# Attention states by one VectorE scan over single-chunk products, in place of two partial sums

## The chip, the core and the metric

The kernel runs on one core of a Trainium2 chip. The metric is the device time of one execution in microseconds. The kernel before takes 101.39 us, the median of three runs (101.31 to 101.42).

## The reference, cut to what matters

Two stages follow each other: a causal linear attention with decay over 32 heads (4 batches of 8), and a token mixer over its output. The change touches only the attention's running state.

```python
batch, n_heads, seq, head_dim = (4, 8, 768, 64)
block = 64
...
for b in range(nb):
    qb, kb, vb = q[:, :, sl], k[:, :, sl], v[:, :, sl]
    intra = (einsum(qb, kb) * Dmask) @ vb
    inter = einsum('bhid,bhde->bhie', qb * lam_pow, kv_state)
    out[:, :, sl] = intra + inter
    kb_dec = kb * rev_pow
    kv_state = lam_block * kv_state + einsum('bhsd,bhse->bhde', kb_dec, vb)
...
# x: the attention's output as (batch, seq, 512)
wq, wk = x @ w_q, x @ w_k
mixed = ((wq @ wk.T) / 8) @ x
result = relu(mixed) @ w_out
```

The state at a block is a sum over all earlier blocks. The kernel uses chunks of 128 tokens, so a head has 6 chunks, and 5 states are needed: chunk c + 1 reads the sum of the products of chunks 0 to c. The decay is put into q and v as powers of lambda that count from the start of the sequence. No factor then stands between one state and the next: the states are plain prefix sums of the products k^T v.

## The kernel before

Two heads make a pair; pair n has its first head on partitions 0 to 63 and its second on 64 to 127 (`R[0]`, `R[1]`). There are 16 pairs. The whole program is one long list of pieces in a fixed order, each with its operands and PSUM banks; `P.6@3` is the piece P of pair 6 in bank 3, and `:a`, `:v` or `:p` names ScalarE, VectorE or GpSimd. The list sets each engine's order. A cut of it, where the first two of the ten pairs stand (lines joined):

```python
ORDER = """
...
m.0.2@3@0 eh.0.2.0@3:a F.4@4 ek.6@2:a eh.0.2.1@0:v P.6@3 P.5@5 Gp.6@3 eh.0.3.0@1:a S0.6@6 O.0.4@2
Gp.5@5 Mc.0.6@6 ef.4@4:v S1.6@6 eo.0.4@2:a I.6@0 Mm.0.6:v I.5@4 V.5@4 M1.6@6 Aq.7@2 ex.5@4:a
...
"""
```

For a pair the pieces are: A and e turn q and k, S multiplies them into scores, M or Mc with Mm masks them, sv scales v, P makes the products for the states, G or Gp brings them to SBUF as states, I multiplies q with the states, V adds the masked scores times v, ex takes the result out, F and ef turn it. Q, K, Y, m, O with their e pieces are the mixer.

There are two ways to the states. With `Pw` (6 of the 16 pairs: 0 to 4 and 14) TensorE forms all prefix sums: the product of chunk c is added to all states from c on, and G is one copy. With `P` (the other ten pairs) only the first two products are summed so, and apart from them the last three; VectorE then adds the state at place 1 to the last three.

```python
    def states(whole):
        def one(n, o):
            to = PS[:, o, 0 : (NCH - 1) * D].rearrange("e (c f) -> e c f", c=NCH - 1)
            for c in range(NCH - 1):
                end = 2 if c < 2 and not whole else NCH - 1
                for hl in range(2):
                    mm(
                        to[R[hl], c:end, :],
                        fk[n][:, hl, c, :],
                        vn[n][:, hl, c, :].unsqueeze(1).to_broadcast([128, end - c, D]),
                        start=(c == 0), stop=(c == NCH - 2), skip_group_check=True,
                    )
        return one
...
    def added(n, o):
        gs[n] = tsb.tile([128, NCH - 1, D], BF16, tag="gs", name="gs")
        of = PS[:, o, 0 : (NCH - 1) * D].rearrange("e (c f) -> e c f", c=NCH - 1)
        two = small.tile([128, 1, D], F32, tag="two", name="two")
        nc.vector.tensor_copy(out=two, in_=of[:, 1:2, :])
        nc.vector.tensor_copy(out=gs[n][:, 0:2, :], in_=of[:, 0:2, :])
        nc.vector.tensor_tensor(
            out=gs[n][:, 2:, :], in0=of[:, 2:, :],
            in1=two.to_broadcast([128, NCH - 3, D]), op=ALU.add,
        )

    def inter(n, o):
        for c in range(1, NCH):
            for hl in range(2):
                mm(
                    PS[:, o + hl, c * D : (c + 1) * D],
                    qT[n][R[hl], c * CH : (c + 1) * CH],
                    gs[n][R[hl], c - 1, :],
                    start=(c == 1), stop=False, skip_group_check=True,
                )
```

In `mm` the second argument holds the weights and the third streams through. So a pair's P has ten products, five for each head, of 128, 64, 192, 128 and 64 columns. Scaling of v (sv) is on VectorE for seven pairs and on GpSimd for nine. GpSimd also issues the loads. One scan is in the kernel already, at its start, over 128 elements in SBUF:

```python
    nc.vector.tensor_tensor_scan(
        out=ET[:, 0:CH], data0=step, data1=step, initial=0.0, op0=ALU.add, op1=ALU.bypass
    )
```

Of the kernel before, what the change touches and what calls it, by code (L numbers as in the profile page):

```python
# [9 lines left out]
BF16 = mybir.dt.bfloat16  # L10
F32 = mybir.dt.float32
ALU = mybir.AluOpType
ACT = mybir.ActivationFunctionType

B, H, S, D = 4, 8, 768, 64
CH = 128
NCH = S // CH
HD = H * D
DHY = 64
NP = H // 2  # L20
HALF = 3 * CH
N = B * NP
R = (slice(0, 64), slice(64, 128))
# [16 lines left out]
Aq.5@4 Ak.5@5 ek2.0.1@1:v ek2.0.0@0:a Mm.1.4:v Y.0@0 ek.5@5:a eq.5@4 YA.0@0:a YB.0@0:v S1.5@4  # L40
M1.5@4 YC.0@0:a m.0.1@1@2 Pw.4@3 eh.0.1.1@2:a m.0.0@0@6 eh.0.1.0@1:v G.4@3:a Aq.6@2 eh.0.0.1@6:a
I.4@4 eq.6@2 eh.0.0.0@0:a S0.5@6 m.0.3@1@3 M0.5@6 V.4@4 eh.0.3.1@3:a Ak.6@2 ex.4@4:a sv.6:v
m.0.2@3@0 eh.0.2.0@3:a F.4@4 ek.6@2:a eh.0.2.1@0:v P.6@3 P.5@5 Gp.6@3 eh.0.3.0@1:a S0.6@6 O.0.4@2
Gp.5@5 Mc.0.6@6 ef.4@4:v S1.6@6 eo.0.4@2:a I.6@0 Mm.0.6:v I.5@4 V.5@4 M1.6@6 Aq.7@2 ex.5@4:a
Ak.7@3 eq.7@2 O.0.5@6 ek.7@3:v V.6@0 eo.0.5@6:v S1.7@2 S0.7@4 M1.7@2 F.5@6 O.0.0@7 ex.6@0:v
O.0.3@2 eo.0.0@7:a M0.7@4 O.0.1@7 ef.5@6:v F.6@3 sv.8:v eo.0.1@7:a P.7@6 Ak.8@4 ef.6@3:a Gp.7@6
Aq.8@7 P.8@5 ek.8@4:a eq.8@7 I.7@0 V.7@0 Gp.8@5 Aq.9@4 ex.7@0:a eo.0.3@2:v Ak.9@5 S0.8@6 ek.9@5:v
S1.8@2 Mc.0.8@6 F.7@0 eq.9@4 O.0.2@5 ef.7@0:v Mc.1.8@2 Mm.0.8:v Q.1.0@4 eo.0.2@5:a Mm.1.8:v
Q.1.1@2 eQ.1.0@4:a S1.9@4 eQ.1.1@2:a S0.9@0 I.8@6 M1.9@4 Mc.0.9@0 P.9@3 K.1@2 V.8@6 Gp.9@3
eK.1@2:a ex.8@6:a Y.1@2 Mm.0.9:v Ak.10@3 YA.1@2:v YB.1@2:a Aq.10@6 ek.10@3:v YC.1@2:a I.9@0  # L50
eq.10@6 m.1.1@4 m.1.2@2 em.1.1@4:a V.9@0 em.1.2@2:v Aq.11@6 ex.9@0:a P.10@7 eq.11@6 m.1.0@2
S0.10@4 Gp.10@7 m.1.3@0 em.1.0@2:a F.9@6 M0.10@4 Ak.11@7 em.1.3@0:a Aq.12@2 Ak.12@3 ef.9@6:a
ek.11@7:v eq.12@2 S1.11@4 ek.12@3:a S0.11@0 S1.10@6 M0.11@0 O.1.1@2 Mc.1.11@4 M1.10@6 O.1.3@3
eo.1.1@2:a Mm.1.11:v P.11@2 eo.1.3@3:a Ak.13@6 Gp.11@2 Aq.13@7 ek.13@6:a S0.12@4 eq.13@7 I.11@2
I.10@0 Mc.0.12@4 V.11@2 V.10@0 ex.11@2:v O.1.4@4 ex.10@0:a Mm.0.12:v F.8@5 eo.1.4@4:a F.11@0
O.1.5@1 ef.8@5:a ef.11@0:v F.10@0 eo.1.5@1:a S1.13@4 ef.10@0:v S0.13@2 S1.12@6 Mc.0.13@2 M1.13@4
Q.2.0@0 Mc.1.12@6 Q.2.1@1 Mm.0.13:v eQ.2.0@0:a P.13@4 Mm.1.12:v Ak.15@5 eQ.2.1@1:a Gp.13@4 Aq.15@0
ek.15@5:a Ak.14@1 eq.15@0 Aq.14@4 ek.14@1:a sv.15:v K.2@6 Pw.14@0 eK.2@6:a S0.15@2 eq.14@4 P.12@1
Mc.0.15@2 Y.2@5 Gp.12@1 G.14@0:a P.15@4 YB.2@5:v YA.2@5:a I.13@2 S1.15@0 Gp.15@4 S0.14@6 YC.2@5:a
V.13@2 Mc.0.14@6 M1.15@0 O.1.0@4 ex.13@2:a Mm.0.14:v I.15@0 S1.14@6 Mm.0.15:v eo.1.0@4:a I.12@2  # L60
V.12@2 M1.14@6 V.15@0 ex.12@2:a I.14@4 ex.15@0:v m.2.3@6 V.14@4 F.12@2 em.2.3@6:v ex.14@4:a F.15@3
F.13@0 ef.12@2:a ef.15@3:v F.14@1 m.2.1@6 ef.13@0:v ef.14@1:a m.2.0@4 m.2.2@2 em.2.0@4:v O.1.2@0
# [9 lines left out]
def kernel(  # L72
# [11 lines left out]
    nc = tc.nc  # L84
    mm = nc.tensor.matmul

    consts = ctx.enter_context(tc.tile_pool(name="consts", bufs=1))
    stage = ctx.enter_context(tc.tile_pool(name="stage", bufs=N))
    tsb = ctx.enter_context(tc.tile_pool(name="tsb", bufs=4))
    small = ctx.enter_context(tc.tile_pool(name="small", bufs=2))  # L90
    big = ctx.enter_context(tc.tile_pool(name="big", bufs=2))
# [4 lines left out]
    PS = ps.tile([128, 8, HD], F32, name="ps")  # L96
    PSH = PS.bitcast(BF16)
# [42 lines left out]
    def load_wo(_):  # L140
# [28 lines left out]
        out=ET[:, 0:CH], data0=step, data1=step, initial=0.0, op0=ALU.add, op1=ALU.bypass  # L169
    )  # L170
    for at, n in ((CH, CH), (2 * CH, 2 * CH), (4 * CH, 2 * CH)):
        nc.vector.tensor_tensor(
            out=ET[:, at : at + n], in0=ET[:, 0:n],
# [3 lines left out]
    ident = consts.tile([128, 128], BF16, name="ident")  # L177
    nc.vector.tensor_tensor(
        out=ident.rearrange("e (p r) -> e p r", r=2), in0=natural,
# [4 lines left out]
        out=mask1, in0=ET[:, 0:CH], in1=row.to_broadcast([128, CH]), op=ALU.is_ge  # L184
# [4 lines left out]
    for r in range(2):  # L189
        nc.vector.tensor_tensor(  # L190
            out=token[R[r], :], in0=token[R[r], :],
# [5 lines left out]
        out=order.rearrange("e (p r) -> e p r", r=2), in0=natural,  # L197
# [5 lines left out]
        out=E6, in0=ET[:, ::CH], in1=row.to_broadcast([128, NCH]), op=ALU.add  # L203
# [3 lines left out]
    lamv = lam_all.rearrange("p (k l) -> p k l", l=2)  # L207
    for hl in range(2):
        nc.scalar.activation(out=lncol[R[hl], :], in_=lamv[R[hl], :, hl], func=ACT.Ln)
    pw48 = consts.tile([128, H, NCH], F32, name="pw48")  # L210
    mask2 = mask1.unsqueeze(1).unsqueeze(1).to_broadcast([128, 2, 3, CH])
    Dq = [consts.tile([128, S], BF16, name=f"dq{kk}") for kk in range(NP)]
# [18 lines left out]
    qT, kT, pr, gs = {}, {}, {}, {}  # L231
    xnat, xT = {}, {}
# [97 lines left out]
    def masked(a):  # L330
        def one(n, o):
            pr[n, a] = tsb.tile([128, 2, HALF], BF16, tag=f"pr{a}", name="pr")
            nc.vector.tensor_tensor(  # L333
                out=pr[n, a].rearrange("j l (c i) -> j l c i", c=3),
                in0=PS[:, o : o + 2, 0:HALF].rearrange("j l (c i) -> j l c i", c=3),
                in1=mask2,
                op=ALU.mult,
            )

        return one  # L340
# [10 lines left out]
        )  # L351


    def states(whole):
        def one(n, o):
            to = PS[:, o, 0 : (NCH - 1) * D].rearrange("e (c f) -> e c f", c=NCH - 1)
            for c in range(NCH - 1):
                end = 2 if c < 2 and not whole else NCH - 1
                for hl in range(2):
                    mm(  # L360
                        to[R[hl], c:end, :],
                        fk[n][:, hl, c, :],
                        vn[n][:, hl, c, :].unsqueeze(1).to_broadcast([128, end - c, D]),
                        start=(c == 0),
                        stop=(c == NCH - 2),
                        skip_group_check=True,
                    )

        return one

    def summed(n, o, eng):
        gs[n] = tsb.tile([128, NCH - 1, D], BF16, tag="gs", name="gs")
        of = PS[:, o, 0 : (NCH - 1) * D].rearrange("e (c f) -> e c f", c=NCH - 1)
        copy(eng, gs[n], of)

    def added(n, o):
        gs[n] = tsb.tile([128, NCH - 1, D], BF16, tag="gs", name="gs")
        of = PS[:, o, 0 : (NCH - 1) * D].rearrange("e (c f) -> e c f", c=NCH - 1)
# [4 lines that stand above are left out]
            out=gs[n][:, 2:, :],  # L383
            in0=of[:, 2:, :],
            in1=two.to_broadcast([128, NCH - 3, D]),
            op=ALU.add,
        )

    def inter(n, o):
        for c in range(1, NCH):  # L390
            for hl in range(2):
                mm(
                    PS[:, o + hl, c * D : (c + 1) * D],
                    qT[n][R[hl], c * CH : (c + 1) * CH],
                    gs[n][R[hl], c - 1, :],
                    start=(c == 1),
                    stop=False,
                    skip_group_check=True,
                )
# [24 lines left out]
    def flip(n, o):  # L424
        b, kk = divmod(n, NP)
        for c in range(NCH):
            nc.tensor.transpose(  # L427
                PSH[:, o, c * CH : (c + 1) * CH],
                xnat[b][:, c, kk * CH : (kk + 1) * CH],
                order,  # L430
            )

    def flipped(n, o, eng):
# [10 lines left out]
    qk, wkn, YA, YB, rmT = {}, {}, {}, {}, {}  # L444
# [24 lines left out]
            qk[b] = small.tile([128, S], BF16, tag="qk", name="qk")  # L469
        copy(eng, qk[b][:, n * HALF : (n + 1) * HALF], PS[:, o, 0:HALF])  # L470

    def mix_k(b, o, chunks=range(NCH)):
        for c in chunks:
            for r in range(2):
                mm(
                    PS[R[r], o, c * DHY : (c + 1) * DHY],
                    qk[b][:, c * CH + r : (c + 1) * CH : 2],
                    ident[:, R[1 - c // 3]],
                    start=(c == chunks[0]),
                    stop=(c == chunks[-1]),  # L480
                    skip_group_check=True,
                )

    def mix_k_half(b, half, o):
        mix_k(b, o, range(3 * half, 3 * half + 3))
# [47 lines left out]
    def relu(eng, to, of):  # L533
        if eng == "a":
            nc.scalar.activation(out=to, in_=of, func=ACT.Relu, scale=1.0 / 8.0)  # L535
        else:
            nc.vector.tensor_scalar(
                out=to, in0=of, scalar1=1.0 / 8.0, scalar2=0.0, op0=ALU.mult, op1=ALU.max
            )

    def mixed_m(b, dd, o, eng):
        if b not in rmT:
            rmT[b] = big.tile([128, 4, 2, HALF], BF16, tag="rmT", name="rmT")
        relu(eng, rmT[b][:, dd], PS[:, o : o + 2, 0:HALF])

    def mixed_m_half(b, dd, n, o, eng):
        if b not in rmT:
            rmT[b] = big.tile([128, 4, 2, HALF], BF16, tag="rmT", name="rmT")
        relu(eng, rmT[b][:, dd, n], PS[:, o, 0:HALF])
# [40 lines left out]
    def zeros(count, o):  # L590
# [9 lines left out]
        q=load_q, k=load_k, v=load_v, wq=load_wq, wk=load_wk, cw=copy_wq, wo=load_wo, hold=hold, dq=make_dq, dv=make_dv,  # L600
        sv=scale_v, Aq=turn_q, Ak=turn_k, eq=turned_q, ek=turned_k, A4q=turn_q4, A4k=turn_k4,
        e4q=turned_q4, e4k=turned_k4, S0=scores(0), S1=scores(1),
        M0=masked(0), M1=masked(1), Mc=drawn, Mm=masked_late, P=states(False), Pw=states(True), G=summed, Gp=added, I=inter, V=values, ex=attended, F=flip,
        ef=flipped, eg=flipped_half, Q=mix_q, eQ=mixed_q, K=mix_k, eK=mixed_k, Kh=mix_k_half, ek2=mixed_k_half, Y=mix_y, YA=mixed_y, YB=crossed_y(0), YC=crossed_y(1), Qp=mix_q_part, m=mix_m,
        em=mixed_m, eh=mixed_m_half, O=mix_o, eo=mixed_o, Oh=mix_o_half, oh=mixed_o_half, Z=zeros,
    )
    for word in ORDER.split():
        piece, _, eng = word.partition(":")
# [34 lines left out]
```

## Time and profile before

| | before |
|---|---|
| time, median of 3 | 101.39 us |
| span of the profiled execution | 99.9 us |
| TensorE busy | 90.6 us, 1458 products |
| TensorE weight loads | 59.4 us |
| VectorE busy | 74.3 us, 145 instructions |
| ScalarE busy | 65.2 us |
| GpSimd busy | 62.2 us |
| TensorE clock granted, mean | 0.983 |

The profile is of one execution, and its span is a little shorter than the time because it starts at the first recorded instruction. A busy share is an average over stages; the chain of waits, followed back from the last instruction, says which engine sets the end in which stretch. In the tables of groups a row names the source line, the engine, the operation, what it writes and reads, the shapes and the count; then busy us and the mean ns of one; then idle time before it and what ended that. Durations include a start and an end that overlap neighbouring instructions, so the spacing of starts in the timeline tells how long an engine is held.

### The profile page before, as it was taken

How to read it: one execution, taken by the hardware profiler on the slowest of the kernel's cores; microseconds unless marked ns; L12 is line 12 of the kernel's file. 1: busy time of each engine (PE TensorE's matmuls, PEld its weight loads, DVE VectorE, ACT ScalarE, POOL GpSimd, SP SyncE). 2: the span in 40 equal slices, each digit the busy share in tenths (PEclk: the TensorE clock that was granted, in tenths of full speed). 3: DMA queues.
4: the chain of work that ended last, by engine and by line, in shares of the span. 5: the costliest groups of instructions: out<-in, count | busy, mean ns of one | idle time of the engine just before them, and what ended most of it. 6: DMA issues, size and time to landing. Idle time of an engine off the chain costs nothing.

```text
span 99.9 us, 3414 instructions
## 1 busy us (share of the span) xinstructions
PE 90.6 (91%) x1458; PEld 59.4 (59%) x1466; DVE 74.3 (74%) x145; ACT 65.2 (65%) x107; POOL 62.2 (62%) x65
## 2 busy tenths in 40 slices
PE   5999999799998779999999999999999999999930
PEld 3465777678555445757858675866976854434400
DVE  6739596988686996799999899787999964482200
ACT  5585414676877924326798898888978895484440
POOL 5999995889989998999999999940000000000000
PEclk9999999999999966999999999999999999999999
DMA  0999999999999999999999999999910202526782
GB/s 1 98 141 161 164 159 166 161 163 166 164 162 200 173 167 159 165 171 156 164 167 163 163 170 161 162 317 403 361 35 7 105 7 105 210 105 243 282 315 105
DMA packets 67438, 16.60 MB, mean 166 GB/s; under 512 B 63840, under 2 KB 64352, under 8 KB 67424
## 3 DMA queue, kind: packets, MB, share of 16 engines
q0 software_dynamic: 63792, 10.10, 136.8%
q1 hardware_dynamic: 3632, 6.30, 16.8%
q8 instruction: 11, 0.18, 0.7%
q14 instruction: 3, 0.02, 0.1%
HBM read 20.19 MB, written 6.29 MB: 265 GB/s over the span
## 4 chain that ended last, share of the span: by engine, by line
PE 42%; DVE 20%; POOL 20%; DMA 8%; issue 4%; ACT 1%; POOLq 0%; DVEq 0%; ACTq 0%
PE ps L553 18%; DMA fv<-in_v_dram 8%; POOL fk L118 6%; POOL fv L122 6%; POOL fq L114 5%; DVE pr L333 4%; PE ps L360 3%; PE ps L319 3%; DVE fv L240 3%; PE ps L404 3%; PE ps L449 3%; PE ps L524 3%; PE ps L427 2%; DVE pr L349 2%; DVE qT L308 2%
## 5 line engine op out<-in xcount | busy, mean ns | idle before, releaser
L553 PE MATMUL ps<-wo,rmT 128*128 128x512 bf16 x88 | 23.2, 388 | 0.7 <-issue 0.4
L122 POOL DMA_DIRECT2D fv<-in_v_dram x16 | 16.6, 1039 | 2.3 <-DMA fv<-in_v_dram 1.4
L333 DVE TENSOR_TENSOR pr<-ps,mask 128x768 bf16<-128x768 f32 x17 | 16.1, 951 | 1.8 <-PE ps L319 1.8
L235 ACT COPY osb<-ps 128x512 f32<-128x512 f32 x18 | 10.6, 588 | 10.3 <-PE ps L553 10.2
L118 POOL DMA_DIRECT2D fk<-in_k_dram x16 | 16.8, 1049 | 0.3 <-DMA fv<-in_v_dram 0.3
L345 ACT CAST pr<-ps 128x768 bf16<-128x768 f32 x15 | 11.7, 803 | 4.8 <-PE ps L319 4.7
L114 POOL DMA_DIRECT2D fq<-in_q_dram x16 | 14.1, 884 | 0.8 <-POOLq L627 0.8
L553 PEld LDWEIGHTS <-rmT 128*128 128x128 bf16 x96 | 8.6, 99 | 9.7 <-issue 1.3
L240 POOL TENSOR_TENSOR fv<-fv,DvI 128x768 bf16<-128x768 bf16 x9 | 14.0, 1572 | 0.0
L235 ACT CAST xnat<-ps 128x768 bf16<-128x768 f32 x12 | 9.6, 800 | 4.3 <-PE ps L404 4.2
L593 PE MATMUL ps<-blank 128*128 128x128 f32 (+3 forms) x26 | 10.5, 514 | 1.1 <-DVE blank L159 1.1
L308 DVE TENSOR_TENSOR qT<-ps,dq 128x768 bf16<-128x768 bf16 x16 | 8.8, 551 | 1.7 <-PE ps L252 1.5
L349 DVE TENSOR_TENSOR pr<-pr,mask 128x768 bf16<-128x768 bf16 x15 | 9.9, 668 | 0.2
L535 ACT ACTIVATE rmT<-ps 128x768 bf16<-128x768 f32 (+1 forms) x14 | 9.0, 677 | 1.1 <-PE ps L524 0.9
L319 PE MATMUL ps<-qT,kT 64*128 64x128 bf16 x192 | 9.4, 223 | 0.4
L360 PE MATMUL ps<-fv,fk 128*64 128x128 bf16 (+4 forms) x160 | 8.1, 236 | 1.8 <-DVE fv L240 1.3
L252 PE MATMUL ps<-ident,fq 128*64 128x128 bf16 x192 | 8.2, 221 | 0.6 <-DMA fq<-in_q_dram 0.5
L360 PEld LDWEIGHTS <-fk 128*64 128x64 bf16 x160 | 6.4, 114 | 3.9 <-DVE fv L240 1.4
L240 DVE TENSOR_TENSOR fv<-fv,DvI 128x768 bf16<-128x768 bf16 x7 | 7.9, 1134 | 0.7 <-DMA fv<-in_v_dram 0.6
L319 PEld LDWEIGHTS <-kT 64*128 64x128 bf16 x192 | 5.8, 96 | 4.1 <-issue 1.9
L261 PE MATMUL ps<-ident,fk 128*64 128x128 bf16 x192 | 8.2, 221 | 0.0
L404 PE MATMUL ps<-fv,pr 128*128 128x64 bf16 x192 | 8.1, 194 | 0.0
(68 smaller groups left out, 143.8 us busy)
## 6 DMA issues: line engine op xcount, KB each, us to landing
out_dram<-osb SPq DMA_DIRECT2D x24, 256.0 KB, 2.0
fq<-in_q_dram POOLq DMA_DIRECT2D x16, 192.0 KB, 8.0
fk<-in_k_dram POOLq DMA_DIRECT2D x16, 192.0 KB, 8.4
fv<-in_v_dram POOLq DMA_DIRECT2D x16, 192.0 KB, 8.5
wo<-in_moe_w_out_dram POOLq DMA_DIRECT2D x1, 512.0 KB, 9.9
wqk<-in_moe_w_q_dram POOLq DMA_DIRECT2D x1, 64.0 KB, 7.9
wqk<-in_moe_w_k_dram POOLq DMA_DIRECT2D x1, 64.0 KB, 7.6
lam_all<-in_lam_dram SPq DMA_DIRECT2D x1, 4.0 KB, 2.5
```

The source lines that it names most:

```text
L114: nc.gpsimd.dma_start(out=fq[n], in_=rows_q(n))
L118: nc.gpsimd.dma_start(out=fk[n], in_=rows(n, k))
L122: nc.gpsimd.dma_start(out=fv[n], in_=rows(n, v))
L235: return (nc.scalar.copy if eng == "a" else nc.vector.tensor_copy)(out=to, in_=of)
L240: (nc.gpsimd if eng == "p" else nc.vector).tensor_tensor(out=vn[n], in0=fv[n], in1=DvI[:, 2 * kk : 2 * kk + 2, :].unsqueeze(3).to_broadcas ...
L319: mm(PS[:, o + hl, cc * CH : (cc + 1) * CH], kT[n][R[hl], c], qT[n][R[hl], c], start=True, stop=True, skip_group_check=True,)
L333: nc.vector.tensor_tensor(out=pr[n, a].rearrange("j l (c i) -> j l c i", c=3), in0=PS[:, o : o + 2, 0:HALF].rearrange("j l (c i) -> j l c ...
L345: nc.scalar.copy(out=pr[n, a], in_=PS[:, o : o + 2, 0:HALF])
L349: (nc.gpsimd if eng == "p" else nc.vector).tensor_tensor(out=of, in0=of, in1=mask2, op=ALU.mult)
L360: mm(to[R[hl], c:end, :], fk[n][:, hl, c, :], vn[n][:, hl, c, :].unsqueeze(1).to_broadcast([128, end - c, D]), start=(c == 0), stop=(c == ...
L404: mm(PS[:, o + hl, c * D : (c + 1) * D], pr[n, c // 3][:, hl, (c % 3) * CH : (c % 3 + 1) * CH], vn[n][:, hl, c, :], start=False, stop=(c = ...
L553: mm(PS[:, o, :], rmT[b][:, kt].rearrange("f n i -> f (n i)")[:, t * CH : (t + 1) * CH], wo[:, kt, :], start=(kt == 0), stop=(kt == 3),)
```

## The change

For the ten pairs with P, the product of each chunk now goes to its own place alone, and VectorE forms all prefix sums in one instruction. A scan computes state = keep * state + product from element to element along the row. For this the five products of one state element must lie side by side, so the products are written to PSUM with a step of five floats (`e (f c) -> e c f`). `keep` is a row of ones with a zero at every fifth place, where a new sum begins. The states come out in the same order, and the products with q read them with a step of five elements. The aim is to take columns from TensorE and two of three small instructions from VectorE. The order of pieces stays the same, with Ps for P and Gs for Gp.

```diff
+    keep = consts.tile([128, (NCH - 1) * D], F32, name="keep")
+    nc.vector.memset(keep, 1.0)
+    nc.vector.memset(keep[:, :: NCH - 1], 0.0)
...
-    def states(whole):
+    def states(form):
         def one(n, o):
-            to = PS[:, o, 0 : (NCH - 1) * D].rearrange("e (c f) -> e c f", c=NCH - 1)
+            to = PS[:, o, 0 : (NCH - 1) * D]
+            if form == "single":
+                to = to.rearrange("e (f c) -> e c f", c=NCH - 1)
+            else:
+                to = to.rearrange("e (c f) -> e c f", c=NCH - 1)
             for c in range(NCH - 1):
-                end = 2 if c < 2 and not whole else NCH - 1
+                end = NCH - 1
+                if form == "halves" and c < 2:
+                    end = 2
+                if form == "single":
+                    end = c + 1
...
+    def scanned(n, o):
+        gs[n] = tsb.tile([128, NCH - 1, D], BF16, tag="gs", name="gs")
+        scans.add(n)
+        nc.vector.tensor_tensor_scan(
+            out=gs[n].rearrange("e c f -> e (c f)"),
+            data0=keep,
+            data1=PS[:, o, 0 : (NCH - 1) * D],
+            initial=0.0,
+            op0=ALU.mult,
+            op1=ALU.add,
+        )
...
     def inter(n, o):
+        to = gs[n]
+        if n in scans:
+            to = to.rearrange("e c f -> e (c f)").rearrange("e (f c) -> e c f", c=NCH - 1)
...
-                    gs[n][R[hl], c - 1, :],
+                    to[R[hl], c - 1, :],
...
-... P.6@3 P.5@5 Gp.6@3 ...
+... Ps.6@3 Ps.5@5 Gs.6@3 ...
```

The diff also adds a few functions that the order does not call; they issue nothing.

## Prediction before the run

> **What bounds the kernel now.** I read four views in this order: the page's first part, the chain of waits in order of time, the groups of VectorE instructions by form, and the timeline around a few places. The first line of the page says that TensorE is busy nearly all the time, and VectorE three quarters of it:
>
> ```profile
> PE 90.6 (91%) x1458; PEld 59.4 (59%) x1466; DVE 74.3 (74%) x145; ACT 65.2 (65%) x107; POOL 62.2 (62%) x65
> ```
>
> These are averages, so the chain decides. It runs over GpSimd and its loads up to 31.85 us, over VectorE to 35.6, over TensorE to 41.9, over VectorE nearly all the way to 59.9, and over TensorE from 60.9 to the last product at 95.9. The changed pieces (P and Gp in the order list) stand on it in the third, fourth and fifth stretch. Pieces of the chain, as start, length and what:
>
> ```profile
> 35.68 1.02 PE ps L360 x20
> ...
> 46.60 0.16 DVE two L380
> 46.76 0.20 DVE gs L381
> 46.96 0.27 DVE gs L382
> ...
> 62.40 0.38 PE ps L360 x10
> ...
> 63.13 0.21 DVE two L380
> 63.34 0.20 DVE gs L381
> 63.54 0.28 DVE gs L382
> ```
>
> The reader is to see that the same change removes TensorE time where TensorE is the bound (first and fifth piece) and alters VectorE time where VectorE is the bound. The ten pairs are 5 to 13 and 15; pairs 5 and 6 lie near 36 us, 7 to 10 in the VectorE stretch, 11, 13, 12 and 15 in the last one.
>
> The table of VectorE's groups by form (count, then busy us and mean ns of one) gives the costs:
>
> ```profile
> L333 DVE TENSOR_TENSOR pr<-ps,mask 128x768 bf16<-128x768 f32 x17 | 16.1, 951 | 1.8 <-PE ps L319 1.8
> ...
> L382 DVE TENSOR_TENSOR gs<-ps,two 128x192 bf16<-128x192 f32 x10 | 3.5, 346 | 0.0
> L381 DVE CAST gs<-ps 128x128 bf16<-128x128 f32 x10 | 2.8, 280 | 0.0
> L380 DVE COPY two<-ps 128x64 f32<-128x64 f32 x10 | 2.2, 218 | 0.3 <-PE ps L360 0.2
> ...
> L168 DVE TENSOR_TENSOR_SCAN ET<-step 128x128 f32<-128x128 f32 x1 | 0.4, 424 | 0.0
> ...
> L172 DVE TENSOR_TENSOR ET<-ET 128x128 f32<-128x128 f32 x1 | 0.3, 291 | 0.0
> ```
>
> By good luck the old kernel has one scan, at its start, beside an addition of the same size.
>
> [...] scan and addition of 128 elements differ by 424 - 291 = 133 ns, or 1.04 ns an element, which is just what one more pass costs (from the L333 and L382 rows, (951 - 346) / (768 - 192) = 1.05 ns an element). [...] The new products write every fifth float. No run of the kernel before has a product written so, so this stays open. [...] at 33.40 us VectorE's scaling of v took 2.23 us beside a GpSimd scaling begun at 33.30, against 0.95 us elsewhere.
>
> **VectorE, per pair.** Removed are three operations. Their durations overlap the next start, so what counts is the spacing. Here is one pair of the timeline (start, duration):
>
> ```profile
> 47.75 0.21 DVE L380 COPY two<-ps 128x64 f32<-128x64 f32 x1
> 47.88 0.28 DVE L381 CAST gs<-ps 128x128 bf16<-128x128 f32 x1
> 48.08 0.35 DVE L382 TENSOR_TENSOR gs<-ps,two 128x192 bf16<-128x192 f32 x1
> 48.35 0.68 DVE L235 COPY osb<-ps 128x512 f32<-128x512 f32 x1
> ```
>
> So they hold VectorE for 48.35 - 47.75 = 0.60 us, and the last is done 0.68 us after the first starts. Added is one scan of 320 elements from PSUM. The fixed part from PSUM is 346 - 192 x 1.05 = 144 ns; two passes of 320 elements are 320 x 2.1 = 672 ns; together 0.82 us. It overlaps its successor as the addition does, by 0.35 - 0.27 = 0.08, so it holds VectorE for 0.74 us. The scan is therefore **0.14 us dearer** than the three operations, although there are two instructions fewer: 1.4 us over ten pairs, and the states come 0.14 us later. In addition there are two fills of the constant at the start: a fill of 128 floats takes 165 ns and of one float 59 ns, so 320 and 64 floats are an estimate of 0.32 + 0.11 us. They stand ahead of VectorE's first wait for loads; gaps of 1.18, 1.02 and 0.60 us before 18 us swallow them, so I count nothing.
>
> **TensorE, per pair.** Ten products remain ten. Their columns fall from 2 x (128 + 64 + 192 + 128 + 64) = 1152 to 2 x 5 x 64 = 640. In the PE-bound stretch a block of ten takes 0.28 us from its start at 69.91 to the next operation's start at 70.19. Twelve products of 64 columns with weights of the same shape (L475) start at 71.53 and are followed at 71.76: 19 ns each. Ten would take 0.19 us, so I expect 0.17 to 0.19 if the step in PSUM costs nothing: **0.1 us saved** a pair, 1.0 us in all. The products that read the states now read every fifth bf16 element. They come in ten for 0.16 us already (76.13 to 76.29), close to how fast 64-column products are issued at all, so I expect little there.
>
> **The sum along the chain.** Pairs 5 and 6: in the windows view the granted clock is 0.50 from 36 to 39 us. Twenty products took 36.63 - 35.68 = 0.95 us; 0.2 x 1.5 to 0.2 x 2 = 0.3 to 0.4 us go. Work that moves forward stays in the half-clock stretch, so about half is kept: -0.2. VectorE's later part has slack there (0.86 us idle before 39.43). Pairs 7 to 10 on VectorE: +0.14 each, +0.56. But the two late maskings from 50.47 took 2.29 us together, against 0.55 each undisturbed. If they wait for GpSimd, which does not move, the 0.28 us of pairs 7 and 8 are absorbed, leaving +0.28. I take +0.45. Pair 11: VectorE sets the start of its readers at 63.86, so +0.14 and no gain from its products. Pairs 12, 13 and 15: products on TensorE's chain, -0.1 each, -0.3; their scans run beside other work. The sum is -0.2 + 0.45 + 0.14 - 0.3 = +0.1 us. To this I add 0.15 for some cost of the stepped write: 101.39 + 0.25, rounded to **101.6 us**.
>
> **Rivals.** (1) TensorE is the bound and the removed columns come through: ten times 0.1 us, twice that at half clock, some 1.2 us: 100.2 us. For it speaks 91% busy; against it the VectorE pieces on the chain from 42 to 60 us. (2) The stepped write in PSUM slows the products. At two cycles a column 640 columns cost what 1152 do now and the saving is gone, which leaves the VectorE loss, +0.6: 102.0. At four, a block would take about 0.5 us, 0.25 more than now, on six chain pairs +1.5 us and the VectorE loss on top: 103.5. [...] (3) VectorE's delay shifts its meetings with GpSimd: one more of 1.3 us, or one fewer, either way. (4) Another half-clock stretch for TensorE[...]: the one above spans about 3.4 us, so 1.7 us of lost work at most. [...]
>
> **Range and chances.** Rivals 1 and 2 without its extreme span 100.2 to 102.0, rival 3 adds a microsecond upwards or downwards. I say 100.4 to 103.0. Two per cent is 2.03 us: below 99.4 would take all the savings and a lost collision, 0.03; above 103.4 would take the slow write, 0.07; within, 0.90.
>
> **What would show it.** The scan's row should read 10 of about 820 ns; if near 480, [...] VectorE gains 0.2 us a pair. The new products should follow each other in 17 to 19 ns; longer means that the step costs. The chain from 42 to 60 us should still be VectorE, later by 0.3 to 0.6 us at its end, and VectorE should count 18 instructions fewer (20 removed, 2 fills added). I am wrong if the maskings at 50 us change by a microsecond, if the half-clock stretch moves, or if the readers of the stepped states slow down.

## The result and the profile after

The changed kernel takes 102.96 us where the kernel before takes 101.36: ratio 1.0139, 95% interval 1.0093 to 1.0184. Times are medians of all executions; the ratios leave out those in a slower state (mean TensorE clock 0.951 to 0.984 in all but two of them, 0.974 to 1.000 in the others), and where only one execution is left, as in the first timing of experiment 2, there is no ratio. Timed a second time, it gave 1.0113 (1.0066 to 1.016). It is slower by a little over one per cent, within the two per cent that I called the same.

The first line of the page, for the changed kernel:

```profile
PE 91.4 (91%) x1466; PEld 60.4 (60%) x1466; DVE 73.9 (73%) x127; ACT 65.3 (65%) x107; POOL 61.9 (61%) x65
```

TensorE lost 5120 columns (ten times 512), and its busy time shows no saving: 91.4 us against 90.6. The two sums are only roughly comparable, because the trace before lacks the records of eight output products (it has 88 of 96; both kernels load weights 1466 times) and holds a stretch at half clock (0.50 from 36 to 39 us). VectorE has 18 instructions fewer and is busy for about as long as before. The next fence is VectorE's group by form (count, then busy us and mean ns of one, then idle time before it):

```profile
L391 DVE TENSOR_TENSOR_SCAN gs<-keep,ps 128x320 bf16<-128x320 f32 x10 | 8.0, 813 | 0.4 <-PE ps L372 0.3
```

The scan takes 813 ns; 820 was predicted. Next, TensorE's two groups that the change touches, by form: the products of q with the states (all 16 pairs), and those single-chunk products that have 64 columns (100 of the 112 are of the ten pairs):

```profile
L421 PE MATMUL ps<-gs,qT 64*128 64x64 bf16 x160 | 7.0, 225 | 0.2 <-DVE gs L391 0.2
L372 PE MATMUL ps<-fv,fk 128*64 128x64 bf16 x112 | 5.7, 239 | 1.2 <-DVE fv L243 1.2
```

The same rows of the kernel before:

```profile
L360 PE MATMUL ps<-fv,fk 128*64 128x64 bf16 x52 | 5.0, 200 | 0.0
...
L392 PE MATMUL ps<-gs,qT 64*128 64x64 bf16 x160 | 4.8, 192 | 0.1
```

Both became slower per product though their size is the same. In the first group the mean hides two kinds: of the 160 products, 60 belong to pairs with dense states; the median of all is 248 ns against 190 before.

The chain shows where this enters the time. Pieces of the chain after, in order of time:

```profile
59.65 0.68 PE ps L322 x18
...
62.83 0.82 DVE gs L391
63.65 0.04 issue
63.69 0.90 PE ps L421 x20
...
70.25 0.40 PE ps L372 x10
...
76.67 0.46 PE ps L421 x10
77.13 0.17 PE ps L322 x6
77.30 0.36 PE ps L421 x10
...
89.57 7.04 PE ps L616 x32
```

And the corresponding pieces of the chain before:

```profile
59.88 0.68 PE ps L319 x18
...
63.86 0.47 PE ps L392 x20
...
69.98 0.38 PE ps L360 x10
...
76.20 0.25 PE ps L392 x10
76.45 0.17 PE ps L319 x6
76.62 0.32 PE ps L392 x10
...
88.84 7.04 PE ps L553 x32
```

Twenty products that read stepped states hold the chain for 0.90 us, against 0.47. Ten single-chunk products hold it for 0.40, against 0.38 for the ten longer ones before. From the start of the eighteen score products at about 60 us (59.88 before, 59.65 after) to the start of the last run of output products (88.84 and 89.57) the kernel before needs 28.96 us and the changed one 29.92: 0.96 us of loss lie in the stretch in which TensorE mostly sets the pace. The twenty readers are 0.43 us of it, and the two runs of ten readers another 0.25 (0.46 + 0.36 against 0.25 + 0.32). VectorE's scan stands on the chain in this stretch too (at 62.83, and again at 74.78), so not all of it need be TensorE's own.

### The profile page after: what moved, and what is told of

It reads as the page before. It is cut to its first block, busy times and chain, and to the rows that moved or that the text cites. A ratio compares the mean times of both kernels' runs of the same rounds, so it can differ in the third digit from the quotient of the medians.

```text
span 100.6 us, 3410 instructions
## 1 busy us (share of the span) xinstructions
PE 91.4 (91%) x1466; PEld 60.4 (60%) x1466; DVE 73.9 (73%) x127; ACT 65.3 (65%) x107; POOL 61.9 (61%) x65
## 4 chain that ended last, share of the span: by engine, by line
PE 53%; POOL 19%; DMA 8%; DVE 8%; issue 5%; ACT 3%; POOLq 0%; DVEq 0%; ACTq 0%
PE ps L616 22%; DMA fv<-in_v_dram 8%; POOL fk L118 6%; POOL fv L122 6%; POOL fq L114 5%; PE ps L497 4%; PE ps L372 4%; PE ps L421 4%; PE ps L456 4%; PE ps L322 4%; PE ps L433 3%; PE ps L554 2%; PE ps L578 2%; PE ps L255 2%; DVE pr L336 2%
## 5 line engine op out<-in xcount | busy, mean ns | idle before, releaser
L372 PE MATMUL ps<-fv,fk 128*64 128x64 bf16 (+4 forms) x160 | 8.0, 246 | 1.7 <-DVE fv L243 1.2
L322 PE MATMUL ps<-qT,kT 64*128 64x128 bf16 x192 | 8.9, 218 | 0.2
L352 DVE TENSOR_TENSOR pr<-pr,mask 128x768 bf16<-128x768 bf16 x15 | 8.7, 591 | 0.1
L391 DVE TENSOR_TENSOR_SCAN gs<-keep,ps 128x320 bf16<-128x320 f32 x10 | 8.0, 813 | 0.4 <-PE ps L372 0.3
```

The costliest lines, as they stand in the source:

```text
L322: mm(PS[:, o + hl, cc * CH : (cc + 1) * CH], kT[n][R[hl], c], qT[n][R[hl], c], start=True, stop=True, skip_group_check=True,)
L372: mm(to[R[hl], c:end, :], fk[n][:, hl, c, :], vn[n][:, hl, c, :].unsqueeze(1).to_broadcast([128, end - c, D]), start=(c == 0), stop=(c == ...
```

## The experiments

Three theories stood against each other. **Reader:** the stepped read of the states by TensorE costs most of it. **Writer:** the stepped write of the products to PSUM does. **Scan:** the dearer scan on VectorE does. Kernels that leave out a step compute other values; their instructions, sizes and waits are those of the kernel they vary. Ratios are to the kernel before, with 95% intervals.

**1. The changed kernel with a dense read.** The states are read in the order in which they are not stored, so the output differs.

```diff
     def inter(n, o):
         to = gs[n]
-        if n in scans:
-            to = to.rearrange("e c f -> e (c f)").rearrange("e (f c) -> e c f", c=NCH - 1)
```

> The changed kernel (102.96 us), but the products of q with the states read the states without a step (the same number of elements in another order, so the values differ). Reader theory: the stepped read costs TensorE some 0.2 us a pair, so the twenty products of two pairs go back from 0.9 to 0.47 us, their mean duration from 248 to 190 ns, and the time falls by 1 to 1.8 us, to 101.2 to 102.0. Writer theory (the stepped write in PSUM) and scan theory (the 0.14 us dearer scan): no change worth naming, 102.6 to 103.1.

Measured: 101.99 us, ratio 1.0048 (1.0022 to 1.0073). The products' median is back at 190 ns. That speaks for the reader theory: 0.9% of the 1.4% go with this one step, or 0.65% of the 1.1% by the second timing of the changed kernel. The other half of a per cent stays.

**2. The changed kernel with a dense write.** The products of the five chunks stand in five separate blocks, and the scan adds neighbours that are no states.

```diff
-            if form == "single":
-                to = to.rearrange("e (f c) -> e c f", c=NCH - 1)
-            else:
-                to = to.rearrange("e (c f) -> e c f", c=NCH - 1)
+            to = to.rearrange("e (c f) -> e c f", c=NCH - 1)
```

> The changed kernel, but the single-chunk products are written to PSUM without a step, so the scan adds neighbours that are no states (values differ, the work is the same in size). Writer theory: the block of ten products falls from 0.27 us to 0.17 to 0.19 us, mean duration from 239 to 200 ns, and the time by 0.3 to 1 us. Reader theory: the blocks get shorter so too, but the larger loss stays; time 102.3 to 102.9. Scan theory: no change.

> The changed kernel with a dense write and the stepped read, timed once more because the first timing was disturbed. Writer theory: 0.3 to 1 us below the changed kernel, ratio to before 1.004 to 1.011. Reader theory alone: ratio 1.012 to 1.014.

The first timing (105.03 us) gives no ratio. The second gave 102.45 us, ratio 1.0078 (1.0053 to 1.0102). The group by form of the second run shows what the dense write does:

```profile
L369 PE MATMUL ps<-fv,fk 128*64 128x64 bf16 x112 | 4.5, 199 | 0.0
```

The product falls from 239 to 199 ns (198 in experiment 5). So the writer theory is right that the stepped write lengthens the products; its share of the time is below.

**3. The kernel before with the stepped read alone.**

```diff
     def inter(n, o):
+        to = gs[n]
+        if n in ten:
+            to = to.rearrange("e c f -> e (c f)").rearrange("e (f c) -> e c f", c=NCH - 1)
```

> The kernel before (101.36 us) with one part of the change: in the ten pairs the products of q read the states with a step of five elements (values differ). Reader theory: +1 to +2 us, 102.4 to 103.4, the products at 248 ns. Scan and writer theories: 101.3 to 101.6.

Measured: 102.21 us, ratio 1.0081 (1.0057 to 1.0105), products at a median of 248 ns. Without scan and without stepped write, the read alone makes more than half of the loss. It is below the range that I gave (102.4 to 103.4): of some 2 us that ten pairs lose at 0.2 us each, 0.8 reach the end.

**4. The kernel before with the scan alone.** One scan over the old partial sums, in place of the copy, the conversion and the addition; the row `keep` and its two fills are added as in the changed kernel.

```diff
-        two = small.tile([128, 1, D], F32, tag="two", name="two")
-        nc.vector.tensor_copy(out=two, in_=of[:, 1:2, :])
-        nc.vector.tensor_copy(out=gs[n][:, 0:2, :], in_=of[:, 0:2, :])
-        nc.vector.tensor_tensor(out=gs[n][:, 2:, :], ...)
+        nc.vector.tensor_tensor_scan(out=gs[n] as one row, data0=keep, data1=PS[...], ...)
```

> The kernel before with one part of the change: one scan of 320 elements in place of the three VectorE operations, products and reads as before (the values are no states). Scan theory: 0.14 us a pair more on VectorE where it is the bound, 101.9 to 102.8. Reader and writer theories: 101.3 to 101.7, since most of it lies beside TensorE's work.

Measured: 102.03 us, ratio 1.0049 (1.0023 to 1.0075). The scan is a loss of half a per cent by itself.

**5. The changed kernel with neither step.** Edits 1 and 2 together.

> The changed kernel without either step: single-chunk products written densely and read densely by the products of q (values differ; sizes and waits are the same). It shows what the change would give if steps were free. Against the run with dense reads alone (ratio 1.005 to before), writer theory: the ten-product blocks fall to 0.17 to 0.19 us, ratio 0.995 to 1.002. If the stepped write is off the chain: ratio stays at 1.004 to 1.006.

Measured: 101.86 us, ratio 1.0022 (0.9996 to 1.0048). This is the change as it was meant, with free steps. The ratio lies between the two cases that I gave, and its interval reaches into both, so by the time alone the stepped write is not shown to cost anything. Against the scan alone (1.0049) the fewer columns bring 0.3%, but these two intervals overlap as well. The change with free steps is not shown to beat the kernel before, nor to be slower than it. In the timeline of this kernel (start, length, what) a block of ten products is followed after 0.18 us:

```profile
61.96 0.35 PE L369 MATMUL ps<-fv,fk 128*64 128x64 bf16 x10
62.14 0.51 PE L264 MATMUL ps<-ident,fk 128*64 128x128 bf16 x12
```

The same place in the timeline of the changed kernel, where the products are written with a step, has 0.27 us:

```profile
62.09 0.47 PE L372 MATMUL ps<-fv,fk 128*64 128x64 bf16 x10
62.36 0.53 PE L264 MATMUL ps<-ident,fk 128*64 128x128 bf16 x12
```

**6. The steps by themselves.** Groups of 40 products of 64 columns, added behind the end of the kernel before; a constant tile is read with a step, or dense products are written with one.

```diff
+    for i in range(40):
+        mm(PS[:, 4 + i % 2, ...], qT[15][R[i % 2], 0:CH], wide[R[i % 2], 0 : s * D : s], ...)   # s = 1, 2, 3, 4, 5, 8
+    for i in range(40):
+        mm(PS[R[i % 2], 6, 0 : s * D : s], fk[15][...], vn[15][...], ...)                       # s = 1, 2, 4, 5, 8
```

> The kernel before, with groups of 40 extra products of 64 columns after its last one: reads of a bf16 operand with a step of 1, 2, 3, 4, 5 and 8 elements, then writes to PSUM with a step of 1, 2, 4, 5 and 8 floats (the output is not touched; the time is longer by the probe and is not compared). [...] if any step costs, 2 is slow already. For writes, if any step costs the same, 2 to 8 are alike.

The timeline of these groups; a source line stands for a step, in the order above, and the spacing of the starts counts:

```profile
98.75 0.76 PE L621 MATMUL ps<-wide,qT 64*128 64x64 bf16 x40
99.35 0.76 PE L624 MATMUL ps<-wide,qT 64*128 64x64 bf16 x40
99.95 1.08 PE L627 MATMUL ps<-wide,qT 64*128 64x64 bf16 x40
100.86 1.36 PE L630 MATMUL ps<-wide,qT 64*128 64x64 bf16 x40
...
103.02 1.55 PE L633 MATMUL ps<-wide,qT 64*128 64x64 bf16 x37 [0.66 <-issue]
104.33 2.56 PE L636 MATMUL ps<-wide,qT 64*128 64x64 bf16 x40
106.82 1.28 PE L639 MATMUL ps<-fv,fk 128*64 128x64 bf16 x40
107.91 2.31 PE L642 MATMUL ps<-fv,fk 128*64 128x64 bf16 x40
109.99 1.35 PE L645 MATMUL ps<-fv,fk 128*64 128x64 bf16 x40
111.14 1.31 PE L648 MATMUL ps<-fv,fk 128*64 128x64 bf16 x40
112.26 1.31 PE L651 MATMUL ps<-fv,fk 128*64 128x64 bf16 x40
```

Reads: dividing each spacing by the number of products (40, and 37 for the rest of step 5), steps 1 and 2 cost 15 ns a product, step 3 23, step 4 29, step 5 35 and step 8 62 ns, with the clock at 1.00 up to 106.4 us, when only a few of the last group remain. From step 2 to step 8 the cost grows with the length of memory that a read runs over. Steps 1 to 4 are not alike, and step 2 is not slow already, as it would be if any step cost. Writes: the clock was 0.50 from 106.8 to about 110 us, so steps 1 and 2 are compared with each other, 27 and 52 ns, and steps 4 and 5, nearly or wholly at full clock (0.96 from 110 to 111 us, 1.00 after that), with each other: 29 and 28 ns; step 8 has the same mean duration as step 5, 247 ns. At half clock the step of 2 cost nearly double here. At full clock the steps of 4, 5 and 8 are alike, and the 28 to 29 ns of the first two stand against 18 ns for dense products in experiment 5 (ten in 0.18 us). Step 2 at full clock was not run.

**7. The changed kernel again, and with a read of step 2.** The second kernel reads a state from 64 elements with a step of two, other values at the same cost of everything else.

```diff
-                    to[R[hl], c - 1, :],
+                    to[R[hl], 40 * (c - 1) : 40 * (c - 1) + 2 * D : 2] if n in scans else to[R[hl], c - 1, :],
```

> The changed kernel itself, timed again for a narrower interval: ratio to before 1.010 to 1.016. The parts measured alone add up to this: scan +0.5%, fewer columns -0.3%, stepped write +0.3%, stepped read +0.9%, together 1.4%.

> The changed kernel, but the products of q read with a step of two elements in place of five (other elements, so values differ). If what counts is the length of memory that a read runs over, as the probe says (steps 1 and 2 both 15 ns apart, step 5 35 ns), the products last 190 ns and the ratio is that of dense reads, 1.003 to 1.007. If any step costs: 248 ns and 1.010 to 1.016.

Measured: 102.49 us and ratio 1.0113 (1.0066 to 1.016) for the changed kernel, 101.90 us and 1.0028 (1.0007 to 1.0049) with step 2; the products' median there is 189 ns. So a read with a step of two costs no more than a dense one and a step of five does, in the kernel (medians of 189 ns with two, 190 dense, 248 with five) as in the probe (15, 15 and 35 ns a product).

The traces allow a closer comparison. From the start of the twenty readers (63.86 us before) to the start of the last run of output products (88.84), with the clock at 1.00, the kernel before takes 24.98 us, and the changed kernel 25.88 in each of its two profiled executions (63.69 to 89.57, and 63.57 to 89.45). The stepped read alone (experiment 3) takes 25.61, the scan alone 25.16, the change with neither step 25.03, and the changed kernel with a read of step 2 takes 25.23. So 0.63 to 0.65 of the 0.90 us lost there go with the read, whether it is added to the kernel before or taken from the changed one. These are single executions.

No experiment points to a version that beats the kernel before. One with both accesses dense and true sums would need a scan that walks along the five blocks in turn, and was not tried.

## Why the prediction was right or wrong

The measured time lies within the range, near its upper end (102.96, and 102.49 when repeated, against 100.4 to 103.0), but the centre, 101.6, is 0.9 to 1.4 us too low. That the range held is in part luck: its upper microsecond was set aside for VectorE operations that might lengthen beside GpSimd (by 1.3 us, an estimate from one scaling of 2.23 us against 0.95 in the profile before), and what filled it was a slower read, for which the sum had nothing. A table of the terms; one per cent of the kernel before is one microsecond, and the late stretch is the one of about 25 us compared under experiment 7:

| term | predicted | measured, whole time | late stretch | from |
|---|---|---|---|---|
| scan on VectorE | +0.45 +0.14 us | +0.5% | +0.18 us | run 4 |
| fewer columns | -0.2 -0.3 us | -0.3% | -0.13 us | run 5 against run 4 |
| stepped write | +0.15 us | +0.3% | +0.20 us | run 1 (late stretch: step 2 of run 7) against run 5 |
| stepped read | "little" | +0.9%, or +0.8% alone | +0.65 us, or +0.63 us alone | changed kernel against run 1 (late stretch: step 2 of run 7); run 3 |
| sum | +0.25 us | +1.4% | +0.90 us | |

The sums close by construction, since each row starts from the run at which the row above ends; what tests them are the read alone (run 3) and the dense write (run 2). A ratio to the kernel before has an interval of about a quarter of a per cent each way (0.45 for the changed kernel), and a difference of two such ratios, by an estimate from the two intervals, 0.4 to 0.5. So the scan and the read are clear of zero, and the columns and the write, in this order, are not settled by the times. The shares depend on the order in which parts are taken, too: the write comes out at 0.6% when it is taken off the changed kernel first (1.0139 against 1.0078), and the read at 0.6% when it is added to the kernel without steps (1.0078 against 1.0022).

**The scan** was right as a cost: 0.82 us predicted, 813 ns measured, told by the old kernel's one scan of 128 elements. Its share of the time, 0.5%, agrees with the 0.59 us forecast, but in the trace of run 4 it does not all stand where the prediction put it. Of pairs 7 to 10, on which +0.45 was counted, only the scans at 52.66 and 57.34 stand on the chain of run 4, whose stretch from 42 to 51 us lies on TensorE. The scans of pairs 5 and 6 at 36.57 and of two of the last pairs at 73.00 and 74.30, which were expected beside other work, stand on it too. That the totals agree is in part luck.

**The fewer columns** were right in the length of a block where the step is free, though what they are worth in time is not settled: a block is followed after 0.18 us in run 5, where 0.17 to 0.19 was expected.

**The stepped write** was named as the open point and as a rival; what a column would cost there was the author's supposition. At 0.27 us a block, against 0.28 before, it is the milder case of that rival, in which the saving of 0.1 us a pair is gone (28 ns a product in the probe). In the rival's working that made 102.0.

**The stepped read** is the step that failed, where the prediction said that the products come "in ten for 0.16 us already, close to how fast 64-column products are issued at all, so I expect little there". The reasoning took the 16 ns a product of the kernel before, which it held to be close to a limit of issue, for a cushion without asking how slow a stepped read could be. That limit was the author's estimate; the shortest spacing of the probe is 15 ns. With the step of five it is 35 ns a product there, and twenty products are followed after 64.53 - 63.69 = 0.84 us in the changed kernel, against 64.26 - 63.86 = 0.40 before. With 0.2 us for each of the ten pairs there were 2 us at stake, of which 0.6 to 0.9 reach the end. A step of four already costs 29 ns in the probe, in place of 15.

**The chain from 42 to 60 us** did not come out as foretold, and this is a second step that failed. It was TensorE up to 53 us in the profile after, and the score products at 60 us started 0.2 us earlier than before. Two things differ in the two profiled executions: the pair of late maskings that took 2.29 us in the profile before took 1.02 after, and the half-clock stretch from 36 to 39 us is missing (clock 0.50 before, 1.00 after). Together with the slower readers these are the three signs of being wrong that the prediction named. The first two are not shown to be the work of the change, for the kernel before has such a chain as well: in run 6, which is that kernel but for one small fill up to 97 us, the clock is 1.00 from 36 to 39 us, and the chain lies on TensorE from 35.6 to 51.1 us:

```profile
44.69 0.38 PE ps L360 x10
...
45.74 0.26 PE ps L360 x10
45.99 0.25 PE ps L392 x10
```

Its two late maskings took 2.09 us, so they do not make the difference. The half-clock stretch is left as the likelier reason why VectorE set the pace in the profile before, which was not tested. What brings such a stretch is not shown: from 33 to 36 us TensorE was busy for 1.58 us before and for 1.59 after. The prediction had taken one execution's chain for the kernel's. Whether GpSimd makes a VectorE operation longer was not tested either, and how much these differences hide of the loss before 63 us stays open; the comparison of times does not rest on them.

## What to carry to other kernels

Before you write a result interleaved so that one instruction can walk along it, price the other engine's access: here one scan saved two instructions and cost TensorE a slower write and a slower read of ten products each (0.27 us for ten written with the step against 0.18 for dense ones, 0.84 us for twenty reads against 0.40). Count a scan at two passes of its length, as the two lengths that were run show: 424 ns for 128 elements, as long as an addition of 256, and 813 ns for 320. Here that makes it dearer than the three short operations that it replaces, although there are two instructions fewer: 320 elements twice hold VectorE for 0.74 us (from its start at 45.76 to the next at 46.50), the 384 elements of the three for 0.60. A stepped access is worth a measurement of 40 products before a change is built on it.

## What the runs showed of the hardware

The cost of a stepped read of TensorE's moving operand (the one that streams through) went with the memory that it covers, for the steps of 2 to 8 elements that were run. A product of 64 bf16 elements with a step of s covers 128 s bytes. Products come in twos, one for each half of the partitions, and two of them take 46, 59 and 71 ns at steps of 3, 4 and 5 (384, 512 and 640 bytes) and 124 ns at step 8 (1024 bytes). That is about 0.11 to 0.12 ns a byte, with a floor of 30 ns, which steps 1 and 2 both show. It is a fit to one execution of the probe.

Stepped writes to PSUM were slower than dense ones: dense products of 64 columns follow each other after 18 ns (run 5), those written with a step of 4 or 5 floats after 28 to 29 ns (run 6), and a step of 8 has the same mean duration as 5, 247 ns. At half clock a step of 2 takes 52 ns against 27 (run 6).
